# Opening three output tile pairs with products that need no forms, in a fused attention and gMLP kernel

## The chip, the cores and the metric

The kernel runs on one core of one Trainium2 chip. The metric is the time of one execution on the device in microseconds (us). TensorE is PE in the profile, VectorE is DVE, ScalarE is ACT, GpSimd is POOL, and SyncE is SP, whose queue issues most DMAs.

## The reference, cut to what matters

A layer-normalised dilated window attention comes first (its result, with the input added, is h), and then a gated MLP with a spatial product. The change touches the second block only.

```
z  = gelu(LN(h) @ w_in)                 # 2048 x 3584
z1 = z[:, :1792];  z2 = LN(z[:, 1792:])
g  = w_sp @ z2 + b_sp[:, None]          # w_sp 2048 x 2048, g 2048 x 1792
out = h + (z1 * g) @ w_out              # w_out 1792 x 1024
```

## The kernel before, in words

**Two halves.** The output's 2048 rows are worked in two halves (`pr` 0 and 1), each of 1024 rows. A half has two stages. The spatial stage (loop over `i`, L1454) makes z1 * g for seven feature tiles of 256 features and stores it in `zg`. The output stage (loop over `q`, L1584) multiplies `zg` by w_out for four pairs of 128-row tiles; `w` counts the pairs over both halves, so the first half has pairs 0 to 3.

**Seven products for eight.** Both stages use the Strassen-Winograd scheme: a product of two 2x2 block matrices by seven block products. For the output stage, A is `zg` (a11, a12, a21, a22: two row tiles by even and odd 128-feature groups) and B is the scaled w_out (B11, B12, B21, B22: even and odd feature groups by the two column halves). Two of the products need no forms, a11*B11 and a12*B21. The others need sums of blocks made by VectorE first: the S forms of a pair (`s_form`, L1437; S1 = a21+a22, S2 = S1-a11, S3 = a11-a21, S4 = a12-S2) and, once for all pairs, the T forms of the weights (`wform`, L1428; T1 = B12-B11, T2 = B22-T1, T3 = B22-B12 written over B12, T4 = B21-T2). Each block product is seven matmuls of 512 columns (`times`, L1272) into a PSUM bank. There are eight banks: two under the name `banka`, six under `bank`. The S forms share five buffers with the z forms, which are the same sums in the spatial stage (`z_form`).

**A pair.** In the pairs that run in seven products, PE makes k1 = a11*B11, k4 = S3*T3, k3 = S1*T1, k2 = S2*T2 in this order (L1627). ScalarE copies k1, k4 and k3 to SBUF as p1, p7 and p5 (L1636). PE then adds a12*B21 to k1, a22*T4 to k4 and S4*B22 to k3 (L1638 to L1641). So each of these three banks is written again after its copy. GpSimd adds p5 to p7 (L1643); VectorE makes the next pair's S forms, then u = k2 + p1 (L1662). GpSimd adds u to p7 (L1670). VectorE turns u into p1 and p5, with the row scale and the residual rows `hr` (L1671, L1672), and makes the four quarters of the output (L1680, L1683, L1685, L1693), which SP stores. I call these seven VectorE instructions the outputs. Between them stands work for the second half: the scaling of its two spatial weight tiles, 2 and 3 (`scale_raw`, L1175, half a tile at a time), and its forms (`t_forms`).

**Pair 0 of the first half.** It is the exception: at the start of the output stage no T forms exist, so it is made of eight products, four banks with 14 matmuls each (L1601 to L1606). VectorE makes all T forms and the S forms of pair 1 beside them and then four outputs (L1616). The last two feature groups of each bank come at the end, because tile 6 of the spatial stage is only just done.

**What comes ahead of it.** The seven weight tiles of w_out are scaled in place (`wout_scaled`, L1411). Tile 0 is scaled in spatial tile 5, after a matmul (`spread`, L1552) that spreads one factor over all partitions; tiles 1 to 4 are scaled by ScalarE and 5 and 6 by VectorE in spatial tile 6. Spatial tile 6 also scales both halves of spatial weight tile 2 on VectorE (L1533, L1534).

**What sets the order.** The order on every engine from here on is the order of the program's lines: each engine takes its own instructions strictly in that order, and semaphores hold it where data or a buffer is not ready.

Of the kernel before, what the change touches and what calls it, by code (L numbers as in the profile page):

```python
# [22 lines left out]
P = 128  # L23
# [109 lines left out]
def kernel(  # L133
# [1277 lines left out]
    def wout_scaled(fp):  # L1411
        w_ = wout_a[:, 2 * fp:2 * fp + 2, :] if fp < 4 else wout_b[:, 2 * fp - 8:2 * fp - 6, :]
        if fp < 5:
            A.activation(w_.bitcast(FP16), w_, ACTF.Copy, scale=kf[:, fp:fp + 1])
        else:
            V.tensor_scalar(w_.bitcast(FP16), w_, kf[:, fp:fp + 1], None, op0=ALU.mult)
# [18 lines left out]
    sforms = {}  # L1435
# [12 lines left out]
    for pr in range(NCH // 2):  # L1448
# [5 lines left out]
        for i in range(NQ):  # L1454
# [50 lines left out]
            if pr == 0:  # L1505
                if 1 <= i <= 4:
                    for t in (TPP + 2 * i - 2, TPP + 2 * i - 1):
                        row_sum(t, 0)
                        row_sum(t, 1)
                if i <= 3:  # L1510
                    load_wn2(TPP + 2 * i)
                for f in WSUM.get(i, ()):
                    wout_sum(f)
                if i == 6:
                    for fp in range(1, 5):
                        wout_scaled(fp)
            more = i + 1 < NQ
            if more:
                if n in (0, NQ):
                    z_form(n + 1, 3)  # L1520
                    z_form(n + 1, 1)
                if n == NQ:
                    bias_rows(1)
                if n == 0:
                    V.memset(ones[:], 1.0)
                    feature_scales()
            elif pr == 1:
                for m in (3, 1, 2, 4):
                    s_form(TPC, m, 0, NQ - 1)
            else:  # L1530
                for fp in range(5, NQ):
                    wout_scaled(fp)
                scale_raw(2, 0)  # L1533
                scale_raw(2, HK)  # L1534
# [13 lines left out]
            if n:  # L1548
                times(k3[:], slab(zs[n, 4]), slab(b22), False)
            if pr == 0 and i == 5:  # L1550
                spread = bank()
                T.matmul(spread[:, 0:2], ones[:], kb[0:1, 2:4], start=True, stop=True)  # L1552
            if more and n not in (0, NQ):
                z_form(n + 1, 3)
# [3 lines left out]
            if more and n not in (0, NQ):  # L1558
                z_form(n + 1, 1)
            if n == 3:  # L1560
                load_wout(4)
            nc.gpsimd.tensor_tensor(z22, p7[:], u[:], op=ALU.add)
            V.tensor_tensor(z21, k4[:], p1[:], op=ALU.add)
# [8 lines left out]
            if more and n not in (0, NQ):  # L1572
# [11 lines left out]
        for q in range(TPC):  # L1584
# [9 lines left out]
            if pr == 0 and q == 0:  # L1594
# [3 lines left out]
                wT12 = wtile([P, 2, NQ, CH], "woutT", "wB")[:].bitcast(FP16)  # L1598
                T1, T2 = pieces(wT12[:, 0]), pieces(wT12[:, 1])
                T4 = pieces(p2.tile([P, NQ, CH], FP16, name="wT4", tag="wn", bufs=1)[:])  # L1600
                accs = [(t, nh, bank_a() if (t, nh) == (0, 0) else bank()) for nh in (1, 0) for t in range(2)]  # L1601
                for f0, f1 in ((0, NF - 2), (NF - 2, NF)):
                    for t, nh, acc in accs:
                        for f in range(f0, f1):
                            T.matmul(acc[:], zg[:, f, (c1, c2)[t]:(c1, c2)[t] + P], wout_tile(f).bitcast(FP16)[:, nh * CH:(nh + 1) * CH],  # L1605
                                     start=(f == 0), stop=(f == NF - 1))  # L1606
                wform(T1, B12, B11)
                wform(T2, B22, T1)
                for m in (3, 1, 2, 4):
                    s_form(1, m)  # L1610
# [3 lines left out]
                for t, nh, acc in accs:  # L1614
                    hr, r_ = (h1, h2)[t], (r1, r2)[t]
                    V.scalar_tensor_tensor(hr[:, nh * CH:(nh + 1) * CH], acc[:], r_, hr[:, nh * CH:(nh + 1) * CH], op0=ALU.mult, op1=ALU.add)  # L1616
                for t, hr in ((t1_, h1), (t2_, h2)):
                    dma(out2d[t * P:(t + 1) * P, :], hr[:])
                continue
# [4 lines left out]
            p1, p7, p5, u = f32("p1", 3), f32("p7"), f32("p5"), f32("u2")  # L1624
            k1, k4, k3, k2 = bank_a(), bank(), bank(), bank()
# [4 lines left out]
            if q == 0:  # L1630
                for k_, a_, b_, _ in prods:
                    times(k_[:], a_, wslab(b_), True, 0, NQ - 1, NQ)
            for k_, a_, b_, p_ in prods:
                times(k_[:], a_, wslab(b_), True, NQ - 1 if q == 0 else 0, NQ, NQ)
                if p_ is not None:
                    A.copy(p_[:], k_[:])  # L1636
            cut = 3 * P
            times(k1[:], a12, wslab(B21), False, 0, NQ, NQ)  # L1638
            times(k4[:], a22, wslab(T4), False, 0, NQ, NQ)
            for lo, hi in ((0, cut), (cut, CH)) if end else ((0, CH),):  # L1640
                times(k3[:, lo:hi], S4, lambda k, lo=lo, hi=hi: wslab(B22)(k)[:, lo:hi], False, 0, NQ, NQ)  # L1641
# [27 lines left out]
            elif pr == 0:  # L1669
                nc.gpsimd.tensor_tensor(p7[:], p7[:], u[:], op=ALU.add)  # L1670
                V.scalar_tensor_tensor(p1[:], u[:], r1, h1[:, CH:D], op0=ALU.mult, op1=ALU.add)  # L1671
                V.scalar_tensor_tensor(p5[:], u[:], r2, h2[:, 0:CH], op0=ALU.mult, op1=ALU.add)  # L1672
# [6 lines left out]
            if pr or q < 3:  # L1679
                V.scalar_tensor_tensor(h1[:, 0:CH], k1[:], r1, h1[:, 0:CH], op0=ALU.mult, op1=ALU.add)  # L1680
            if pr == 0 and q < 3:
                (lambda: scale_raw(3, 0), lambda: t_forms(1, 0))[q - 1]()
# [9 lines left out]
            else:  # L1692
                V.scalar_tensor_tensor(h1[:, CH:D], k3[:], r1, p1[:], op0=ALU.mult, op1=ALU.add)  # L1693
                for t, hr in ((t2_, h2), (t1_, h1)):
                    dma(out2d[t * P:(t + 1) * P, :], hr[:])
            if pr == 0 and q == 1:
                scale_raw(3, HK)
# [32 lines left out]
```

## Time and profile before

| | us |
|---|---|
| median of 3 runs | 689.83 |
| lowest, highest | 689.65, 689.96 |
| profiled execution | 689.65 |
| its span in the trace | 687.9 |
| PE busy | 680.6 (99%) |
| DVE busy | 586.5 (85%) |
| ACT busy, POOL busy | 357.6, 170.2 |
| spatial stage of the first half, output stage of the first half | about 427 to 513, 513 to 557 |
| spatial and output stage of the second half | about 557 to 641, 641 to 685 |

In rows in order of time the columns are start, duration, engine, line, operation, what is written from what, its shape, and in square brackets how long the engine sat idle just before and who released it. A matmul's row is longer than its share of PE's time, because matmuls overlap: 379 ns is shown for one of 512 columns, and the next starts 216 ns after it. VectorE's rows overlap a little too, so I use the distance from one start to the next. The granted clock of PE is full throughout.

### The profile page before, as it was taken

To read this page: it belongs to the slowest core of one execution; us is meant where nothing else is said; L and a number is where in the kernel's file an instruction comes from. 1 tells how busy PE (TensorE), PEld (TensorE's weight loads), DVE (VectorE), ACT (ScalarE), POOL (GpSimd) and SP (SyncE) were. 2 spreads that over 40 slices of the span, in tenths; PEclk is the share of its full clock that TensorE was granted. 3 is DMA by queue.
4 is the path that set the end of the run, shared out by engine and by line. 5 is a ranking of instruction groups with operands and counts; after the bars stand their busy time and mean duration, and the time that the engine had idled before them with its cause. 6 is when DMAs were issued, how large, how long until landed. Compare 5 with 4: busy or idle time off the path is not lost.

```text
span 687.9 us, 9194 instructions
## 1 busy us (share of the span) xinstructions
PE 680.6 (99%) x3430; PEld 361.2 (53%) x3447; DVE 586.5 (85%) x742; ACT 357.6 (52%) x527; POOL 170.2 (25%) x145
## 2 busy tenths in 40 slices
PE   9999999999999999999999999999999999999997
PEld 6766666566645445444544467444444444444443
DVE  6899899998999989998897878997789999555565
ACT  4547652354229998764882556387771122324121
POOL 0100010010210101000120134474550426453442
PEclk9999999999999999999999999999999999999999
DMA  8979588567995469454483996999968215542031
GB/s 321 332 240 246 173 193 274 154 165 269 218 352 216 96 244 238 166 174 106 123 225 120 204 275 195 299 295 310 257 189 215 88 62 150 156 121 94 1 114 70
DMA packets 143933, 133.07 MB, mean 193 GB/s; under 512 B 68752, under 2 KB 115504, under 8 KB 143760
## 3 DMA queue, kind: packets, MB, share of 16 engines
q1 hardware_dynamic: 132720, 88.93, 45.1%
q0 software_dynamic: 8416, 34.80, 17.9%
q10 hardware_dynamic: 2752, 8.75, 3.8%
q8 instruction: 27, 0.44, 0.3%
q14 instruction: 18, 0.15, 0.1%
HBM read 75.25 MB, written 33.10 MB: 158 GB/s over the span
## 4 chain that ended last, share of the span: by engine, by line
PE 93%; DVE 2%; issue 2%; DMA 1%; POOL 1%; ACT 0%; DVEq 0%; POOLq 0%
PE bank L1274 22%; PE acc L468 22%; PE acc L800 14%; PE acc L868 11%; PE banka L1274 9%; PE acc L723 8%; PE acc L310 2%; PE acc L1040 1%; PE bank L1605 1%; DMA wout_a<-in_B_w_out_dram 1%; DVE zs L1209 1%; PE wps L232 1%; PE banka L1605 0%; PE banka L1040 0%; PE L L562 0%
## 5 line engine op out<-in xcount | busy, mean ns | idle before, releaser
L800 PE MATMUL acc<-win,hnT 128*128 128x512 bf16 (+1 forms) x501 | 97.4, 352 | 0.6
L800 PEld LDWEIGHTS <-hnT 128*128 128x128 bf16 x512 | 49.9, 98 | 47.4 <-issue 0.7
L532 DVE TENSOR_TENSOR prod<-qT,kT 128x4096 bf16<-128x4096 bf16 x32 | 72.7, 2282 | 1.6 <-ACT kT L474 1.3
L868 PE MATMUL acc<-hnT,win 128*128 128x512 bf16 x336 | 73.7, 379 | 0.0
L1274 PEld LDWEIGHTS <-zs 128*128 128x128 f16 x448 | 43.7, 98 | 54.4 <-DVE zs L1209 2.2
L479 ACT CAST stg<-acc 128x1024 bf16<-128x1024 f32 x36 | 36.4, 1012 | 61.6 <-PE acc L468 54.7
L468 PE MATMUL acc<-xnT,wk 128*128 128x512 bf16 x256 | 56.5, 379 | 0.0
L468 PE MATMUL acc<-xnT,wv 128*128 128x512 bf16 x256 | 56.4, 380 | 0.0
L723 PE MATMUL acc<-wo_sb,av_oT 128*128 128x512 bf16 x250 | 55.8, 379 | 0.3
L868 PEld LDWEIGHTS <-win 128*128 128x128 bf16 x336 | 32.7, 98 | 39.3 <-issue 0.5
L1274 PEld LDWEIGHTS <-z 128*128 128x128 bf16 x336 | 32.7, 98 | 39.1
L1274 PE MATMUL bank<-rawb,zs 128*128 128x512 f16 x224 | 52.6, 379 | 0.0
L1274 PE MATMUL bank<-form,zs 128*128 128x512 f16 x224 | 51.0, 379 | 1.2 <-DVE zs L1209 1.2
L1274 PE MATMUL banka<-rawa,z 128*128 128x512 f16 x224 | 52.0, 379 | 0.0
L468 PEld LDWEIGHTS <-wk 128*128 128x128 bf16 x256 | 36.5, 143 | 19.0 <-issue 0.8
L468 PEld LDWEIGHTS <-wv 128*128 128x128 bf16 x256 | 36.5, 144 | 18.6 <-issue 0.5
L468 PE MATMUL acc<-xnT,wq 128*128 128x512 bf16 x192 | 41.9, 379 | 0.0
L723 PEld LDWEIGHTS <-av_oT 128*128 128x128 bf16 x256 | 24.9, 98 | 29.9
L807 ACT ACTIVATE u<-acc 128x1024 bf16<-128x1024 f32 (+1 forms) x32 | 29.2, 911 | 19.6 <-PE acc L800 19.4
L536 DVE TENSOR_TENSOR prod<-prod 128x2048 bf16<-128x2048 bf16 x32 | 38.7, 1215 | 0.0
L1504 POOL TENSOR_TENSOR p<-p,p 128x512 f32<-128x512 f32 x14 | 22.4, 1602 | 53.6 <-ACT p L1488 48.5
L468 PEld LDWEIGHTS <-wq 128*128 128x128 bf16 x192 | 27.5, 143 | 13.9
(327 smaller groups left out, 1235.8 us busy)
## 6 DMA issues: line engine op xcount, KB each, us to landing
z<-z_d SPq DMA_DIRECT2D x28, 512.0 KB, 5.1
qkv_d<-stg SPq DMA_DIRECT2D x36, 256.0 KB, 4.7
wn<-in_B_w_sp_dram ACTq DMA_DIRECT2D x16, 512.0 KB, 5.1
z1c<-z_d SPq DMA_DIRECT2D x14, 512.0 KB, 4.8
z_d<-z1s SPq DMA_DIRECT2D x21, 256.0 KB, 2.6
z_d<-u SPq DMA_DIRECT2D x12, 448.0 KB, 2.6
av_y<-av_z POOLq DMA_DIRECT2D x4, 1024.0 KB, 9.8
av_oT<-av_zz POOLq DMA_DIRECT2D x4, 1024.0 KB, 15.1
```

The source lines that it names most:

```text
L232: T.matmul(wps[:], warm[:, 0:P], warm[:], start=True, stop=True)
L310: T.matmul(dst.rearrange("p (a b) -> p a b", b=P), wqs[:, kt, dl, :], xnT[0][:, lo:hi, kt, :], start=start, stop=stop)
L468: T.matmul(G[key][:, j, :].rearrange("p (a b) -> p a b", a=TPC), wv[:, kt, dl, :], xnT[c][:, :, kt, :], start=(kt == 0), stop=(kt == KT - 1))
L479: A.copy(stg[:], G[key][:])
L532: V.tensor_tensor(st["prod"][:], qT[:], kT[:, :, o:o + CH], op=ALU.mult)
L536: V.tensor_tensor(dst, p_[:, 0:4, :], p_[:, 4:8, :], op=ALU.add)
L723: T.matmul(st["acc", il][:, nh, :], oTs[c][:, dl, il * P:(il + 1) * P], wo_sb[:, dl, nh * CH:(nh + 1) * CH], start=(dl == 0), stop=(dl == ...
L800: T.matmul(accf[:, n0:n1], hnTs[c][:, il, kt, :], wins[hf][:, kt, n0:n1], start=(kt == 0), stop=(kt == KT - 1))
L807: A.activation(st["u", il][:, hf * 1024:hf * 1024 + wd], G["accz", c, il, hf][:].rearrange("p a b -> p (a b)")[:, 0:wd], ACTF.Gelu_apprx_t ...
L868: T.matmul(G["accy", c, fp][:, j, :].rearrange("p (a b) -> p a b", a=TPC), wt[:, kt, f0 * P:(f0 + 1) * P], hnTs[c][:, :, kt, :], start=(kt ...
L1274: T.matmul(dst, wts(k), mov(k), start=(first and k == 0), stop=(k == last - 1), skip_group_check=not first)
L1504: nc.gpsimd.tensor_tensor(p7[:], p7[:], p5[:], op=ALU.add)
```

## The change

Pair 0 of the first half is made of seven products like the others. To give PE something to do while the T forms are made, a11*B11 and a12*B21 of pairs 0, 1 and 2 run first (42 matmuls, three banks that stay open, with three copies p1); the last feature tile of a11*B11 comes after the first six of all three. Pair 0 then runs S1*T1, S2*T2, S4*B22, S3*T3, a22*T4; pairs 1 and 2 leave out the two products that they already have; pair 3 is as it was.

The rest moves around it. VectorE makes half of T1 (the part of w_out in the second buffer) inside spatial tile 6. Weight tile 4 is scaled by VectorE. The scaling of spatial weight tile 2 leaves spatial tile 6 and goes between the outputs of pair 0; those of tile 3 stay in pair 1. In each pair of the first half one quarter of the output moves between the making of p1 and p5. In spatial tile 5 the `spread` matmul goes ahead of a product, and in spatial tile 1 one z form, (2, 2) of the next tile, goes ahead of two other instructions.

```diff
@@ -1410,7 +1410,7 @@
 
     def wout_scaled(fp):
         w_ = wout_a[:, 2 * fp:2 * fp + 2, :] if fp < 4 else wout_b[:, 2 * fp - 8:2 * fp - 6, :]
-        if fp < 5:
+        if fp < 4:
             A.activation(w_.bitcast(FP16), w_, ACTF.Copy, scale=kf[:, fp:fp + 1])
         else:
             V.tensor_scalar(w_.bitcast(FP16), w_, kf[:, fp:fp + 1], None, op0=ALU.mult)
@@ -1432,7 +1432,8 @@
     def wslab(b):
         return lambda k: b[0][:, k, :] if k < 4 else b[1][:, k - 4, :]
 
-    sforms = {}
+    sforms, opened = {}, {}
+    NOPEN = 3
 
     def s_form(u, m, lo=0, hi=NQ):
         x0 = (u % TPC) * 2 * P
@@ -1512,7 +1513,7 @@
                 for f in WSUM.get(i, ()):
                     wout_sum(f)
                 if i == 6:
-                    for fp in range(1, 5):
+                    for fp in range(1, 4):
                         wout_scaled(fp)
             more = i + 1 < NQ
             if more:
@@ -1528,10 +1529,8 @@
                 for m in (3, 1, 2, 4):
                     s_form(TPC, m, 0, NQ - 1)
             else:
-                for fp in range(5, NQ):
+                for fp in range(4, NQ):
                     wout_scaled(fp)
-                scale_raw(2, 0)
-                scale_raw(2, HK)
             if n + 2 < 2 * NQ:
                 load_z2f(n + 2, 1)
             if n == 5:
@@ -1545,11 +1544,11 @@
             nc.gpsimd.tensor_tensor(u[:], u[:], bt2, op=ALU.add)
             if pr == 0 and i == 5:
                 wout_turned(turned[0:1, P:2 * P])
-            if n:
-                times(k3[:], slab(zs[n, 4]), slab(b22), False)
             if pr == 0 and i == 5:
                 spread = bank()
                 T.matmul(spread[:, 0:2], ones[:], kb[0:1, 2:4], start=True, stop=True)
+            if n:
+                times(k3[:], slab(zs[n, 4]), slab(b22), False)
             if more and n not in (0, NQ):
                 z_form(n + 1, 3)
             z11, z12 = zg[:, 2 * i, 0:CH], zg[:, 2 * i, CH:2 * CH]
@@ -1557,9 +1556,15 @@
             V.tensor_tensor(z11, k1[:], bt1, op=ALU.add)
             if more and n not in (0, NQ):
                 z_form(n + 1, 1)
+            if n == 1:
+                z_form(n + 1, 2)
             if n == 3:
                 load_wout(4)
             nc.gpsimd.tensor_tensor(z22, p7[:], u[:], op=ALU.add)
+            if n == NQ - 1:
+                wT12 = wtile([P, 2, NQ, CH], "woutT", "wB")[:].bitcast(FP16)
+                T1, T2 = pieces(wT12[:, 0]), pieces(wT12[:, 1])
+                wform(T1, wblk(0, 1), wblk(0, 0), (1,))
             V.tensor_tensor(z21, k4[:], p1[:], op=ALU.add)
             if more and n in (0, NQ):
                 z_form(n + 1, 4)
@@ -1569,7 +1574,7 @@
             if n not in Z1ACT:
                 z1_scaled(n)
             V.tensor_tensor(z12, k3[:], u[:], op=ALU.add)
-            if more and n not in (0, NQ):
+            if more and n not in (0, 1, NQ):
                 z_form(n + 1, 2)
             V.tensor_tensor(zg[:, 2 * i, :], zg[:, 2 * i, :], z1c[:, 0, :], op=ALU.mult)
             if more and n not in (0, NQ):
@@ -1595,50 +1600,58 @@
                 load_raw(3)
                 bias_in(1)
                 load_z1c(NQ + 1)
-                wT12 = wtile([P, 2, NQ, CH], "woutT", "wB")[:].bitcast(FP16)
-                T1, T2 = pieces(wT12[:, 0]), pieces(wT12[:, 1])
                 T4 = pieces(p2.tile([P, NQ, CH], FP16, name="wT4", tag="wn", bufs=1)[:])
-                accs = [(t, nh, bank_a() if (t, nh) == (0, 0) else bank()) for nh in (1, 0) for t in range(2)]
-                for f0, f1 in ((0, NF - 2), (NF - 2, NF)):
-                    for t, nh, acc in accs:
-                        for f in range(f0, f1):
-                            T.matmul(acc[:], zg[:, f, (c1, c2)[t]:(c1, c2)[t] + P], wout_tile(f).bitcast(FP16)[:, nh * CH:(nh + 1) * CH],
-                                     start=(f == 0), stop=(f == NF - 1))
-                wform(T1, B12, B11)
+                zz = zg[:].rearrange("p (k j) s -> p j k s", j=2)
+                first = [slab(zz[:, j, :, 2 * v * P:(2 * v + 1) * P]) for v in range(NOPEN) for j in range(2)]
+                for v in range(NOPEN):
+                    opened[v] = bank_a() if v < 2 else bank(), f32("p1", 3)
+                for lo, hi in ((0, NQ - 1), (NQ - 1, NQ)):
+                    for v in range(NOPEN):
+                        times(opened[v][0][:], first[2 * v], wslab(B11), True, lo, hi, NQ)
+                        if hi == NQ:
+                            A.copy(opened[v][1][:], opened[v][0][:])
+                for v in range(NOPEN):
+                    times(opened[v][0][:], first[2 * v + 1], wslab(B21), False, 0, NQ, NQ)
+                wform(T1, B12, B11, (0,))
+                s_form(0, 1)
                 wform(T2, B22, T1)
-                for m in (3, 1, 2, 4):
-                    s_form(1, m)
+                for m in (2, 4, 3):
+                    s_form(0, m)
                 wform(B12, B22, B12, (0,))
                 wform(B12, B22, B12, (1,))
                 wform(T4, B21, T2)
-                for t, nh, acc in accs:
-                    hr, r_ = (h1, h2)[t], (r1, r2)[t]
-                    V.scalar_tensor_tensor(hr[:, nh * CH:(nh + 1) * CH], acc[:], r_, hr[:, nh * CH:(nh + 1) * CH], op0=ALU.mult, op1=ALU.add)
-                for t, hr in ((t1_, h1), (t2_, h2)):
-                    dma(out2d[t * P:(t + 1) * P, :], hr[:])
-                continue
             zz = zg[:].rearrange("p (k j) s -> p j k s", j=2)
             a11, a12, a22 = slab(zz[:, 0, :, c1:c1 + P]), slab(zz[:, 1, :, c1:c1 + P]), slab(zz[:, 1, :, c2:c2 + P])
             S1, S2, S3, S4 = (slab(sforms[w, m]) for m in (1, 2, 3, 4))
             T3 = B12
-            p1, p7, p5, u = f32("p1", 3), f32("p7"), f32("p5"), f32("u2")
-            k1, k4, k3, k2 = bank_a(), bank(), bank(), bank()
+            k1, p1 = opened[w] if w in opened else (bank_a(), f32("p1", 3))
+            p7, p5, u = f32("p7"), f32("p5"), f32("u2")
+            k4, k3, k2 = bank(), bank(), bank()
             end = w == NT // 2 - 1
             prods = [(k1, a11, B11, p1), (k4, S3, T3, p7), (k3, S1, T1, p5), (k2, S2, T2, None)]
             if end:
                 prods = [prods[n_] for n_ in (0, 3, 2, 1)]
-            if q == 0:
+            elif w in opened:
+                prods = [prods[n_] for n_ in ((2, 3, 1) if w == 0 else (1, 2, 3))]
+            cut = 3 * P
+            def three():
+                for lo, hi in ((0, cut), (cut, CH)) if end else ((0, CH),):
+                    times(k3[:, lo:hi], S4, lambda k, lo=lo, hi=hi: wslab(B22)(k)[:, lo:hi], False, 0, NQ, NQ)
+
+            if w == TPC:
                 for k_, a_, b_, _ in prods:
                     times(k_[:], a_, wslab(b_), True, 0, NQ - 1, NQ)
             for k_, a_, b_, p_ in prods:
-                times(k_[:], a_, wslab(b_), True, NQ - 1 if q == 0 else 0, NQ, NQ)
+                if w == 0 and k_ is k4:
+                    three()
+                times(k_[:], a_, wslab(b_), True, NQ - 1 if w == TPC else 0, NQ, NQ)
                 if p_ is not None:
                     A.copy(p_[:], k_[:])
-            cut = 3 * P
-            times(k1[:], a12, wslab(B21), False, 0, NQ, NQ)
+            if w not in opened:
+                times(k1[:], a12, wslab(B21), False, 0, NQ, NQ)
             times(k4[:], a22, wslab(T4), False, 0, NQ, NQ)
-            for lo, hi in ((0, cut), (cut, CH)) if end else ((0, CH),):
-                times(k3[:, lo:hi], S4, lambda k, lo=lo, hi=hi: wslab(B22)(k)[:, lo:hi], False, 0, NQ, NQ)
+            if w:
+                three()
             if not end:
                 nc.gpsimd.tensor_tensor(p7[:], p7[:], p5[:], op=ALU.add)
             if q + 1 < TPC:
@@ -1669,6 +1682,10 @@
             elif pr == 0:
                 nc.gpsimd.tensor_tensor(p7[:], p7[:], u[:], op=ALU.add)
                 V.scalar_tensor_tensor(p1[:], u[:], r1, h1[:, CH:D], op0=ALU.mult, op1=ALU.add)
+                if q < 3:
+                    V.scalar_tensor_tensor(h1[:, 0:CH], k1[:], r1, h1[:, 0:CH], op0=ALU.mult, op1=ALU.add)
+                else:
+                    V.scalar_tensor_tensor(h1[:, CH:D], k3[:], r1, p1[:], op0=ALU.mult, op1=ALU.add)
                 V.scalar_tensor_tensor(p5[:], u[:], r2, h2[:, 0:CH], op0=ALU.mult, op1=ALU.add)
             else:
                 A.activation(p1[:], u[:], ACTF.Copy, scale=r1)
@@ -1676,10 +1693,10 @@
                 nc.gpsimd.tensor_tensor(p1[:], p1[:], h1[:, CH:D], op=ALU.add)
                 nc.gpsimd.tensor_tensor(p5[:], p5[:], h2[:, 0:CH], op=ALU.add)
                 nc.gpsimd.tensor_tensor(p7[:], p7[:], u[:], op=ALU.add)
-            if pr or q < 3:
+            if pr:
                 V.scalar_tensor_tensor(h1[:, 0:CH], k1[:], r1, h1[:, 0:CH], op0=ALU.mult, op1=ALU.add)
             if pr == 0 and q < 3:
-                (lambda: scale_raw(3, 0), lambda: t_forms(1, 0))[q - 1]()
+                (lambda: scale_raw(2, 0), lambda: scale_raw(3, 0), lambda: t_forms(1, 0))[q]()
             V.scalar_tensor_tensor(h2[:, 0:CH], k4[:], r2, (u if end else p5)[:], op0=ALU.mult, op1=ALU.add)
             if not end:
                 V.scalar_tensor_tensor(h2[:, CH:D], p7[:], r2, h2[:, CH:D], op0=ALU.mult, op1=ALU.add)
@@ -1690,11 +1707,12 @@
                     V.scalar_tensor_tensor(h1[:, CH + lo:CH + hi], k3[:, lo:hi], r1, p1[:, lo:hi], op0=ALU.mult, op1=ALU.add)
                     (dma if n else A.dma_start)(out2d[t1_ * P:(t1_ + 1) * P, CH + lo:CH + hi], h1[:, CH + lo:CH + hi])
             else:
-                V.scalar_tensor_tensor(h1[:, CH:D], k3[:], r1, p1[:], op0=ALU.mult, op1=ALU.add)
+                if pr or q < 3:
+                    V.scalar_tensor_tensor(h1[:, CH:D], k3[:], r1, p1[:], op0=ALU.mult, op1=ALU.add)
                 for t, hr in ((t2_, h2), (t1_, h1)):
                     dma(out2d[t * P:(t + 1) * P, :], hr[:])
-            if pr == 0 and q == 1:
-                scale_raw(3, HK)
+            if pr == 0 and q < 2:
+                scale_raw(2 + q, HK)
     sp_hand.__exit__(None, None, None)
     by_hand.__exit__(None, None, None)
```

## The prediction, made before the result

> **What bounds the kernel now.** I read the page's busy shares first, then the slices, then PE's own rows in order of time from 400 us to the end, and last the rows of VectorE between 513 and 575 us.
>
> ```profile
> PE 680.6 (99%) x3430; PEld 361.2 (53%) x3447; DVE 586.5 (85%) x742; ACT 357.6 (52%) x527; POOL 170.2 (25%) x145
> PE   9999999999999999999999999999999999999997
> DVE  6899899998999989998897878997789999555565
> ```
>
> PE has work in every slice, so a matmul taken out is time won only if PE does not wait instead. VectorE is full in slices 30 to 33 (516 to 585 us): the four output pairs of the first half and the start of the second half. After that it is half idle. So in just the stretch that the change rearranges two engines are full. PE waits there for nothing, but only because VectorE is a few us ahead. The waits view has one wait of PE from 390 us to the end:
>
> ```profile
> PE bank L1274 <- DVE zs L1209: 1.2, 1, 1.2
> ```
>
> Four groups of rows carry the sums. First, PE: 28 matmuls of a pair from 525.26 to 531.31 us, so 0.216 us each and 1.51 for a product of seven.
>
> ```profile
> 525.26 1.03 PE L1274 MATMUL banka<-wout_a,zg 128*128 128x512 f16 x4
> 531.31 1.03 PE L1274 MATMUL banka<-wout_a,zg 128*128 128x512 f16 x4
> 556.99 7.07 PE L1274 MATMUL banka<-rawa,z 128*128 128x512 f16 x32
> ```
>
> Second, the time from a product's last matmul to the next one in the same bank, with ScalarE's copy between them (first pair of the second half): last matmul starts 646.78, copy 647.20 to 647.78, next matmul 647.83, so 1.05 us from start to start.
>
> ```profile
> 646.78 0.38 PE L1274 MATMUL banka<-wout_b,zg 128*128 128x512 f16 x1
> 647.20 0.58 ACT L1636 COPY p<-banka 128x512 f32<-128x512 f32 x1 [11.66 <-PE banka L1274]
> 647.83 0.59 PE L1274 MATMUL banka<-wout_a,zg 128*128 128x512 f16 x2
> ```
>
> Third, VectorE's prices. Start to start, which is what a queue pays, a 2048-column weight form costs 1.14, a 1536-column one 0.87, four S forms 2.4, one output instruction 0.66, half a spatial tile (L1178) 2.2.
>
> ```profile
> 516.38 1.21 DVE L1430 TENSOR_TENSOR woutT<-wout_a 128x2048 f16<-128x2048 f16 x1
> 517.52 0.94 DVE L1430 TENSOR_TENSOR woutT<-wout_b 128x1536 f16<-128x1536 f16 x1
> 505.99 4.48 DVE L1178 TENSOR_TENSOR rawa<-rawa,rows 128x4096 f16<-128x4096 bf16 x2
> 543.42 1.14 DVE L1446 TENSOR_TENSOR sf<-zg 128x896 f16<-128x896 f16 x2
> ```
>
> Fourth, GpSimd beside it: of two equal instructions the one that meets GpSimd's add takes 1.75 us in place of 0.75.
>
> ```profile
> 534.02 0.75 DVE L1671 SCALAR_TENSOR_TENSOR p<-u,rinv_w,hr 128x512 f32<-128x512 f32 x1
> 534.13 1.77 POOL L1670 TENSOR_TENSOR p<-p,u 128x512 f32<-128x512 f32 x1 [1.96 <-DVE u L1662]
> 534.69 1.75 DVE L1672 SCALAR_TENSOR_TENSOR p<-u,rinv_w,hr 128x512 f32<-128x512 f32 x1
> ```
>
> **The change part by part.** Clock times are those of the profile before; the earlier gap is taken off at the end.
>
> *Matmuls.* Pair 0 takes 56 matmuls now and 49 after: 7 x 0.216 = **-1.51**.
>
> *The gap.* PE stands 1.18 us before 457.39, for z form (2,2) of L1209, which VectorE starts at 456.18. Moved up in tile 1 it follows form (2,1) and is done near 454.7; PE wants it at 456.2. **-1.18**. What is late next there: nothing, form (2,4) is ready 459.6 and wanted near 461.4. The sum over the tile z21 slips by 0.6, and VectorE has idle time in tiles 3 to 5.
>
> *Small moves.* The spread matmul goes ahead of eight others; its input is written by 497.61 and PE is there at 499.15, so no wait, and VectorE loses 0.82 idle, ScalarE starts scaling 0.8 sooner. Weight tile 4 goes from ScalarE (1.99) to VectorE (0.70): VectorE then ends at 506.8 and its next input, k2, is there at 508.2, so it is hidden; tile 4 is wanted by PE at 514. Scaling of spatial tile 2 (4.4) leaves tile 6, so u and GpSimd's three adds there run up to 2 us sooner, but zg still waits for PE's last product (ends 513.2): by the second half's same tile (product starts 639.87, z12 at 641.87, then two multiplications) zg is done at 515.45, not 516.4. The first T form's second part fits in VectorE's idle time before it. No DMA moves, except that outputs and the loads of hr behind them on SP shift with VectorE; hr(4), loaded behind pair 0's output near 541, is wanted near 553.
>
> *New waits of PE.* In the opening, two single matmuls follow a product's last one before the same bank is written again: 1.05 - 3 x 0.216 = **+0.40**. In pair 0, a22*T4 follows S3*T3 in the same bank at once: 1.05 - 0.216 = **+0.83**. Both are bounded below by 0 and above by 1.05.
>
> *VectorE's queue, the term that decides.* PE, never short of forms: opening 513.18 to 522.64 (42 matmuls and 0.40), pair 0 to 531.02 (35 and 0.83), pair 1 to 538.58, pair 2 to 546.1; pair 3 opens with a product that needs no forms and wants S3 at **547.7**. VectorE, from 515.45: rest of T1 1.14, S1 0.6, T2 2.0, three S forms 1.8, T3 2.0, T4 2.0 = 525.0. Three S forms of pair 1 end at 526.8. The fourth takes the buffer of pair 0's S4 (five buffers), which PE reads until 527.2, so 527.95. Then u, p1, h1's first half: 529.95. The next one, p5, writes what GpSimd's add reads, and that add waits for the copy of S3*T3 (529.47) and takes 1.2: p5 ends near 531.5. Half of tile 2 2.2; three outputs 2.0, the middle one behind GpSimd's second add (+0.6); the other half 2.2, with GpSimd's add for pair 1 in its way (+0.4): about 538.9. S3 of pair 2 is ready at 539.5, wanted at 538.58: **+0.9**. The next round (four S forms 2.4, seven outputs 4.6, two halves of tile 3 4.4 = 11.4, and one block of 0.5 and one of 0.5 by GpSimd) ends at 551.3, S3 of pair 3 is there at **551.9**; six products follow, 9.07, and the next row's matmuls (556.99 now) start at 561.0. That is **+4.0**, in which the -1.51, +0.40, +0.83 and +0.9 are contained and a second stall of about 3.4.
>
> Why so much: the queue before runs without idle from 516.4 to 574 and gets 8.8 us more (tile 2 4.4, four S forms 2.4, seven outputs for four 2.0), less 0.87 and 0.95 of a sooner start, while PE arrives sooner. Before, S3 of pair 3 was ready at 544.0 and wanted at 547.93: 3.9 us of lead, which does not cover it. Behind 561.0 both shift alike (forms of tile 8 were 1.2 ahead and still are), and from 588 us VectorE idles, so the loss is kept and does not grow.
>
> GpSimd's share is bounded both ways. Without a single block: the bare prices sum to 548.2 for S3 of pair 3, and the two waits by data (0.65 for the buffer, 0.85 for p5) make it 549.7. With each of its four adds in full (1.1 each, as 1.75 against 0.75 shows): 553. I take 551.9, because before each pair paid for both adds, and one output now stands between p1 and p5 in the add's way. The Trainium skill, page SBUF — State Buffer, section Who interferes with whom, says that GpSimd and a VectorE instruction with two SBUF inputs hold the shared port pair exclusively for a whole instruction, so the second blocks. The 1.75 beside the 1.77 above agrees; by that rule h1's half, with one input in PSUM, runs free beside the add, and a pair pays nearer 0.5 than 1.0 for it, which would put the end at the lower half of my bounds.
>
> **Sum.** 689.65 (profiled execution; its span is 687.9) + 4.0 - 1.18 = 692.5. The median of the runs shown is 0.18 above that execution, and I forecast on the median's scale: **692.6**.
>
> **The rivals.**
> *VectorE keeps ahead* (the other side, faster). PE then only has -1.51 - 1.18 + 0.40 + 0.83 = -1.46: 688.4. It decides if S3 of pair 3 is done by 547.7, 4.2 us sooner than I walk. For it: PE had no wait here before, and seven outputs may pack tighter with the new order. Against it: bare prices alone give 548.2.
> *VectorE is late, but GpSimd hardly blocks.* S3 at 549.7: 558.8 for the next row, +1.8 - 1.18 = +0.6, 690.4. For it: h1's half between p1 and p5. Against it: the adds still fall beside S forms and scalings, as a 4.40 us add at 541.29 shows.
> *The change does not do what it says at tile 1*: z form (2,2) is still late (ScalarE's copies run 1 us behind there, and GpSimd's adds lengthen forms to 1.04): the 1.18 stays, 693.8; with all adds in full, 695.
>
> **How the numbers follow.** The forecast, 691.2 to 694.4, has 0.59; the little-blocked queue, 688.5 to 691.2, 0.25; VectorE ahead, under 688.5, 0.12; more than 694.4, 0.04. A measurement of this kernel tells about 0.2% (1.4 us) from no change. So faster 0.12, same 0.25, slower 0.63. The range leaves out most of the faster case and the far end: 688.9 to 694.4.
>
> **What would show it.** PE's waits should name DVE sf L1446's form twice, near 538 and near 548 to 552, the second the longer; a wait of 0.8 for ScalarE's copy ahead of a22*T4 in pair 0; none at 457. VectorE should have no idle from 531 to 575. The row matmuls behind the four pairs should start near 560, against 556.99. I am wrong if PE does not wait before pair 3, or if VectorE idles while PE waits.

## The result and the profile after

The changed kernel takes **695.10 us** (median of 4 runs, 694.82 to 695.43), the kernel before 689.74 beside it (4 runs, 689.35 to 689.96). The ratio is 1.0079, 95% interval 1.0061 to 1.0096: 5.4 us slower. The direction was forecast, the size was not: 692.6 was forecast, and 695.10 is above the range. The profiled execution took 695.43 us with a span of 693.7, so 5.78 us more than the profiled execution before; the rows below explain that difference.

The page's busy shares and slices after:

```profile
PE 682.1 (98%) x3440; PEld 360.9 (52%) x3440; DVE 591.8 (85%) x750; ACT 357.2 (51%) x529; POOL 167.6 (24%) x147
...
PE   9999999999999999999999999999999799999997
...
DVE  6899899998999899998896878996989999555565
```

PE has a hole in slice 31, counted from 0 (538 to 555 us, of 17.3 each), where before it had none, though it was given less work. VectorE's slices look much as they did. A share of 85% hides that its work there has grown: its z form (8, 3) for the second half starts at 576.03, where it started at 570.63 before. PE's waits after 390 us, from the waits view (total, times, longest):

```profile
PE bank L1274 <- DVE sf L1447: 5.3, 2, 3.8
PE bank L1274 <- ACT p L1649: 0.7, 1, 0.7
PE banka L1274 <- ACT p L1612: 0.2, 1, 0.2
```

The wait of 1.2 for a z form is gone, and the forecast waits are there: the two for ScalarE's copies, and S3 twice, the second time the longer. The output stage's first row before, and then PE's rows after in order of time:

```profile
513.18 1.89 PE L1605 MATMUL bank<-wout_a,zg 128*128 128x512 f16 x8
```

```profile
511.90 1.03 PE L1274 MATMUL banka<-wout_a,zg 128*128 128x512 f16 x4
...
516.84 1.02 PE L1274 MATMUL banka<-wout_a,zg 128*128 128x512 f16 x4 [0.24 <-ACT p L1612]
...
528.25 1.67 PE L1274 MATMUL bank<-wT,zg 128*128 128x512 f16 x7 [0.67 <-ACT p L1649]
...
538.97 1.04 PE L1274 MATMUL bank<-wout_a,sf 128*128 128x512 f16 x4 [1.49 <-DVE sf L1447]
...
552.02 1.47 PE L1274 MATMUL bank<-wout_a,sf 128*128 128x512 f16 x4 [3.81 <-DVE sf L1447]
...
554.56 3.85 PE L1274 MATMUL bank<-woutT,sf 128*128 128x512 f16 x14
558.25 1.03 PE L1274 MATMUL banka<-wout_a,zg 128*128 128x512 f16 x4
...
562.78 7.07 PE L1274 MATMUL banka<-rawa,z 128*128 128x512 f16 x32
```

Read the starts. The output stage begins at 511.90, 1.28 sooner than before (513.18). The next row's matmuls begin 50.88 later, at 562.78, where they took 43.81 before. What was not forecast stands in the durations at 552.02 and 554.56: four matmuls in 1.47 where 1.03 is usual. From 552.02 to 558.25 PE runs 21 matmuls, at 0.216 each 4.54 us; it takes 6.23. The view by stretches (busy time of PE, PEld, DVE, ACT and POOL with counts, then PE's granted clock, DMA share, GB/s) shows it:

```profile
552.00:554.00 2.00, 1.98 (x6) 0.77 (x7) 1.79 (x4) 0.00 (x0) 0.00 (x0) 0.62 0.62 234
554.00:556.00 2.00, 2.00 (x6) 0.72 (x5) 1.96 (x4) 0.59 (x1) 1.30 (x1) 0.53 0.00 0
556.00:558.00 2.00, 2.00 (x11) 0.88 (x9) 2.00 (x3) 0.59 (x1) 0.87 (x2) 1.00 0.00 0
```

Behind the wait the granted clock is 0.62 and 0.53, and the view counts 6 matmuls in 2 us where it counts 11 at full clock (those that reach into a stretch are counted in it). So the wait is paid once as a wait and then again, 1.69 us, as a slow restart. The Trainium skill, page TensorE: Matmul & The Clock Gate, section What's actually happening, says that PE falls to half clock after an idle window of about 3.4 us and that this window runs freely. The 0.53 here agrees with the half; the length of wait that it takes is tested below.

The terms, start to start, on PE's clock of the profiled executions:

| term | forecast | measured |
|---|---|---|
| matmuls of pair 0 | -1.51 | -1.51 |
| copy wait in the opening (516.22 to 516.84, less 0.216) | +0.40 | +0.40 |
| copy wait in pair 0 | +0.83 | +0.83 |
| S3 of pair 2 (pair 1 ends 537.31, row at 538.97) | +0.9 | +1.66 |
| S3 of pair 3 (product before it ends 548.04, row at 552.02) | +3.4 | +3.98 |
| clock behind that wait | none | +1.69 |
| sum, 513.18 or 511.90 to the next row | +4.0 | +7.05 (rows: 50.88 - 43.81 = +7.07) |
| gap in spatial tile 1 and what lies ahead of the output stage | -1.18 | -1.28 |

7.07 - 1.28 is 5.79, the 5.78 of the profiled executions. Nothing is lost or won behind 562.78.

VectorE's side, its rows with GpSimd's beside them:

```profile
528.28 1.26 POOL L1656 TENSOR_TENSOR p<-p,p 128x512 f32<-128x512 f32 x1 [16.17 <-ACT p L1649]
529.57 1.86 DVE L1689 SCALAR_TENSOR_TENSOR p<-u,rinv_w,hr 128x512 f32<-128x512 f32 x1 [0.79 <-POOL p L1656]
529.62 1.27 POOL L1683 TENSOR_TENSOR p<-p,u 128x512 f32<-128x512 f32 x1
```

```profile
534.22 1.30 DVE L1702 SCALAR_TENSOR_TENSOR hr<-p,rinv_w,hr 128x512 bf16<-128x512 f32 x1
...
542.87 1.09 DVE L1689 SCALAR_TENSOR_TENSOR p<-u,rinv_w,hr 128x512 f32<-128x512 f32 x1
543.89 3.35 DVE L1178 TENSOR_TENSOR rawb<-rawb,rows 128x4096 f16<-128x4096 bf16 x1
...
551.35 1.15 DVE L1447 TENSOR_TENSOR sf<-zg 128x896 f16<-128x896 f16 x2
```

p5 of pair 0 waits 0.79 for GpSimd's add, as forecast (0.85), and then takes 1.86 for 0.75: GpSimd's second add starts 0.05 behind it and takes its usual 1.27, so it seems to go first. Half a tile 3 takes 3.35 for 2.27. An output (at 534.22) takes 1.30 for 0.74 and p5 of pair 1 1.09 for 0.75. These four make 3.1 us of blocking up to pair 3's S forms; I had put 2.0. Those forms start at 551.35 and S3, the first, takes 0.61, so it is written by 551.96.

### The profile page after: what moved, and what is told of

It reads as the page before. It is cut to its first block, busy times and chain, and to the rows that moved or that the text cites. A ratio compares the mean times of both kernels' runs of the same rounds, so it can differ in the third digit from the quotient of the medians.

```text
span 693.7 us, 9215 instructions
## 1 busy us (share of the span) xinstructions
PE 682.1 (98%) x3440; PEld 360.9 (52%) x3440; DVE 591.8 (85%) x750; ACT 357.2 (51%) x529; POOL 167.6 (24%) x147
## 4 chain that ended last, share of the span: by engine, by line
PE 92%; issue 4%; DVE 2%; DMA 1%; POOL 1%; ACT 0%; DVEq 0%; POOLq 0%
PE bank L1274 23%; PE acc L468 22%; PE acc L800 14%; PE acc L868 10%; PE banka L1274 9%; PE acc L723 8%; PE acc L1040 2%; PE acc L310 2%; PE acc L1004 0%; DMA xp<-in_A_x_dram 0%; PE banka L1040 0%; DMA hr<-h_d 0%; DVE rawb L1178 0%; PE L L562 0%; DMA out_dram<-hr 0%
## 5 line engine op out<-in xcount | busy, mean ns | idle before, releaser
L1274 PEld LDWEIGHTS <-sf 128*128 128x128 f16 x231 | 22.6, 100 | 33.4 <-DVE sf L1447 6.3
```

Source lines behind the costliest of these rows:

```text
L1274: T.matmul(dst, wts(k), mov(k), start=(first and k == 0), stop=(k == last - 1), skip_group_check=not first)
```

## The experiments

**Theory A**, formed from these rows: VectorE's queue is the whole loss. It was nearly full, it got more than it can do ahead of pair 3, GpSimd's adds lengthen it, and PE's falling clock adds to the wait that comes of it. The rivals differ from run to run and stand in each expectation: that the seven-product pair is at fault and not the scaling that moved, that the order within VectorE's queue is at fault and not its length, that the blocking by GpSimd matters little.

The medians of the kernel before, beside the runs, were 689.6 (27 runs; beside the gap alone, 14 more matmuls, the scaling back in tile 6, and no GpSimd adds) and 689.39 (7 runs; beside the other four).

### The gap alone

The kernel before with only the z form (2, 2) moved up in spatial tile 1.

```diff
             if more and n not in (0, NQ):
                 z_form(n + 1, 1)
+            if n == 1:
+                z_form(n + 1, 2)
...
-            if more and n not in (0, NQ):
+            if more and n not in (0, 1, NQ):
                 z_form(n + 1, 2)
```

> The kernel before with one edit: z form (2, 2) goes ahead of two instructions in spatial tile 1, and nothing else. Theory A (PE bounds everything there, and the 1.18 us wait is simply gone): 688.4, that is 1.2 to 1.4 us under the kernel before, with no wait of PE from 390 us on. Rival (the time is given back where VectorE has least lead, near spatial tile 8 of the second half, because VectorE's chain there does not start sooner): 689.0 to 689.7, with a new wait of PE near 570 to 590 us.

Measured: 688.12 (687.89 to 688.56, 11 runs), ratio 0.998 (0.9971 to 0.9989). The waits view has no wait of PE from 390 us to the end, and the next row's matmuls start 1.35 sooner than before's 556.99:

```profile
555.64 7.07 PE L1274 MATMUL banka<-rawa,z 128*128 128x512 f16 x32
```

This part of the change does what the prediction said. It is the fastest kernel of the study.

### The clock: 14 more matmuls in the wait, and 7

The changed kernel, with 14 matmuls that repeat a11*B11 into the bank of S3*T3 just ahead of it in pair 3. They change nothing in the output; they only keep PE at work in the wait.

```diff
+                if w == 3 and k_ is k4:
+                    for _ in range(2):
+                        times(k4[:], a11, wslab(B11), True, 0, NQ, NQ)
                 times(k_[:], a_, wslab(b_), True, NQ - 1 if w == TPC else 0, NQ, NQ)
```

> The changed kernel with 14 more matmuls, which only repeat a11*B11 into the bank that S3*T3 of pair 3 overwrites next, so they change no result and stand where PE waits 3.8 us. Theory A (after that wait PE's granted clock is about half for some 3 us, and this costs 1.7 us): with the wait cut to about 0.9 us the clock stays full, 21 matmuls behind it take 4.54 us in place of 6.23, and the time falls by 1.7 to 693.4 although PE does more work. Rival B (the matmuls are slow because the forms S1 and S2 arrive just in time, or because of what the other engines read meanwhile): the same slow matmuls, 695.1 or more.

Measured: 694.64 (694.34 to 694.87), 0.5 less than the change, where A said 1.7 less. PE's rows, and a stretch of the same view as above:

```profile
551.85 1.04 PE L1274 MATMUL bank<-wout_a,sf 128*128 128x512 f16 x4 [0.79 <-DVE sf L1447]
...
556.39 1.03 PE L1274 MATMUL banka<-wout_a,zg 128*128 128x512 f16 x4
...
577.30 1.90 PE L1274 MATMUL bank<-rawb,zs 128*128 128x512 f16 x8 [0.51 <-DVE zs L1209]
```

```profile
552.00:554.00 2.00, 2.00 (x10) 0.88 (x9) 1.79 (x4) 0.43 (x1) 0.00 (x0) 1.00 0.60 201
```

A's mechanism held: with a wait of 0.79 for 3.81 the clock stays at 1.00, the 21 matmuls take 4.54, and the next row's matmuls start at 560.92, 1.86 sooner. But 1.26 of it is given back behind that: 0.16 at a bank that VectorE seems to free late, 0.67 in spatial tile 8, where PE now waits for z form (8, 3), and 0.4 in tile 9 for form (9, 2). So the clock's drop costs 1.7 on the spot and only some 0.6 in the end. Behind it stands VectorE again, 25 us later. This is the first sign that tile 8, and not pair 3, decides. Part of that is GpSimd once more: with PE on time its add starts at 556.26 for 557.60, meets a form of the second half (3.35 for 2.28), and z form (8, 3) starts 0.54 later than in the change.

With 7 matmuls (`range(1)`):

> The changed kernel with 7 more matmuls (as in the run with 14) where PE waits 3.8 us, so that the wait is about 2.3 us. It is for the size of wait at which PE's granted clock drops: waits of 1.5 us left it full, one of 3.8 did not. Theory A (it takes more than 3 us of standing): the 21 matmuls behind the wait take 4.54 us, clock 1.00. Rival (any wait of 2 us does it): about 6 us for them, clock 0.6 or less.

Measured: 694.64 (one run). PE's wait is 2.30 here, and the clock stays full:

```profile
551.66 1.04 PE L1274 MATMUL bank<-wout_a,sf 128*128 128x512 f16 x4 [2.30 <-DVE sf L1447]
```

The 21 matmuls take 4.54 again (551.66 to 556.20), and tiles 8 and 9 take the win back in the same way. A's outcome came here; what it says of the length of wait is taken up again below, where a shorter one did bring the clock down.

### The scaling of spatial tile 2 back in tile 6

The changed kernel with one part undone.

```diff
                 for fp in range(4, NQ):
                     wout_scaled(fp)
+                scale_raw(2, 0)
+                scale_raw(2, HK)
...
-            if pr == 0 and q < 3:
-                (lambda: scale_raw(2, 0), lambda: scale_raw(3, 0), lambda: t_forms(1, 0))[q]()
+            if pr == 0 and 0 < q < 3:
+                (lambda: scale_raw(3, 0), lambda: t_forms(1, 0))[q - 1]()
...
-            if pr == 0 and q < 2:
-                scale_raw(2 + q, HK)
+            if pr == 0 and q == 1:
+                scale_raw(3, HK)
```

> The changed kernel with one part undone: both halves of spatial weight tile 2 are scaled in spatial tile 6 again, as before the change. Theory A (the 4.4 us that this move puts into VectorE's full queue are what PE waits for): S3 of pair 3 is ready near 546.7 against 551.9, PE waits under 1 us in all, no clock drop, the next row's matmuls start near 556 against 562.8, 688.1 to 689.5. Rival (the seven-product pair's own S forms and outputs, 4.4 us more, are already too much for VectorE): waits of 2 us or more remain before pair 2 or 3 or near tile 8, 690.5 to 692.

Measured: 690.82 (690.34 to 691.04, 10 runs), ratio 1.0016 (1.0007 to 1.0025). The rival's number came, not A's. PE's waits:

```profile
PE bank L1274 <- DVE sf L1447: 1.3, 1, 1.3
...
PE bank L1274 <- DVE zs L1209: 0.7, 2, 0.5
```

So the move of 4.4 us of scaling costs 4.3 us (695.10 to 690.82), nearly all of itself. But the rest of the change does not pay either: it is 2.7 above the gap alone. The rows say how. The next row's matmuls start at 557.10, 1.46 behind the gap alone; from there to the product of z form (8, 3) it takes 16.38 for 15.54, and a wait in tile 9, start to start, adds 0.40. Both are VectorE's: a pair in seven products saves PE 1.5 us, gives 0.40 and 0.83 back in copy waits, and puts four S forms and three outputs more, 4.4 us, into VectorE's full stretch. (The other moves of the change are still in this kernel, and none of them was run by itself but the gap and the output quarter.) A's cause holds here, but not its belief that the scaling was all of it.

### The scaling moved alone, in the kernel before

The reverse: the kernel before with pair 0 in eight products, and only the scaling of tile 2 moved, behind pair 0's four outputs.

```diff
-                scale_raw(2, 0)
-                scale_raw(2, HK)
...
                     dma(out2d[t * P:(t + 1) * P, :], hr[:])
+                scale_raw(2, 0)
+                scale_raw(2, HK)
                 continue
```

> The kernel before with one edit: the scaling of spatial weight tile 2 leaves spatial tile 6 and stands behind the four outputs of pair 0, which stays in eight products. Theory A (VectorE's queue from 516 us on is full and had 1.2 us of lead at tile 8): 4.4 us more, less 1.0 for the sooner end of tile 6, less the lead, so PE waits about 2.2 us in all, 691.4 to 692.4. Rival (4.4 us fit into VectorE's lead over PE, and it is the seven products that cost): 689.5 to 690.2.

Measured: 693.0 (692.87 to 693.33), ratio 1.0054 (1.0037 to 1.007): slower, as A said, and by more than it said. No product was taken out and no bank is written sooner, so the new waits are the moved scaling's alone (of the three for z forms one is the old 1.18 in tile 1):

```profile
PE bank L1274 <- DVE zs L1209: 2.6, 3, 1.2
PE bank L1274 <- DVE sf L1446: 1.4, 1, 1.4
```

The z form (8, 3) and the row of PE that holds its product, before (the product is the second eight of the row) and here:

```profile
570.63 0.67 DVE L1209 TENSOR_TENSOR zs<-z 128x1024 f16<-128x1024 bf16 x1
570.81 3.62 PE L1274 MATMUL bank<-rawb,zs 128*128 128x512 f16 x16
```

```profile
574.58 0.68 DVE L1209 TENSOR_TENSOR zs<-z 128x1024 f16<-128x1024 bf16 x1
575.32 1.90 PE L1274 MATMUL bank<-rawb,zs 128*128 128x512 f16 x8 [1.16 <-DVE zs L1209]
```

The form starts at 574.58 for 570.63 before, 3.95 later. In the kernel before it was 1.18 ahead of PE (started 570.63, product at 572.54, and 0.73 from the form's start to the product's where PE waits for it). 3.95 - 1.18 is 2.77, and the product starts 2.78 later, at 575.32. A wait in tile 9, for form (9, 2), adds 0.40: 3.2, which is the difference of the profiled executions (692.87 and 689.65).

### The second halves behind the S forms

The changed kernel with the second halves of tiles 2 and 3 scaled behind the next pair's S forms: the same work in an order that serves PE's nearest need first.

```diff
                     s_form(w + 1, m)
+                if pr == 0 and q in (1, 2):
+                    scale_raw(1 + q, HK)
...
-            if pr == 0 and q < 2:
-                scale_raw(2 + q, HK)
```

> The changed kernel with one reordering on VectorE and the same work: the second half of spatial weight tile 2 is scaled behind the S forms of pair 2, and that of tile 3 behind the S forms of pair 3, instead of ahead of them. Theory A (VectorE's queue as a whole is too long up to the forms of tile 8, at 576 us): PE's wait before pair 2 goes and that before pair 3 shrinks by about the 1.5 us that the earlier one took and more, but a wait for a z form of tile 8 appears, 693.2 to 694.6. Rival (only the order is wrong, there is room behind): 690.5 to 691.5, no wait near 576 us.

Measured: 694.77 (694.65 to 694.85), 0.3 below the change, just above A's range and 3 us above the rival's: that the order is at fault falls. PE's waits did not go, they moved:

```profile
PE bank L1274 <- DVE sf L1447: 2.0, 1, 2.0
PE bank L1274 <- DVE u L1677: 1.1, 1, 1.1
PE bank L1274 <- DVE zs L1209: 0.7, 2, 0.5
...
PE banka L1274 <- DVE hr L1663: 0.4, 1, 0.4
```

S3 comes sooner, but banks are freed later (u and hr are the instructions that read them out). And the z form (8, 3) starts at 576.57, and its product at 577.30: to the hundredth where they start with 14 matmuls in the wait, though PE's waits in pairs 2 and 3 differ between the two.

The clock fell here too, behind a wait of 2.05, shorter than the 2.30 that left it full: the 21 matmuls take 6.30 (549.65 to 555.95).

```profile
552.00:554.00 2.00, 2.00 (x6) 0.71 (x5) 2.00 (x2) 0.37 (x1) 0.00 (x0) 0.50 0.64 211
```

### Without GpSimd's adds

The changed kernel without GpSimd's two adds into p7 in pairs 0 to 2.

```diff
-            if not end:
+            if not end and (pr or q == 3):
                 nc.gpsimd.tensor_tensor(p7[:], p7[:], p5[:], op=ALU.add)
...
-                nc.gpsimd.tensor_tensor(p7[:], p7[:], u[:], op=ALU.add)
+                if q == 3:
+                    nc.gpsimd.tensor_tensor(p7[:], p7[:], u[:], op=ALU.add)
```

> The changed kernel without GpSimd's two adds into p7 in pairs 0, 1 and 2 of the first half, so the last quarter of the output of these pairs lacks p5 and u. Theory A (the adds block VectorE: 0.8 us wait by data, 1.1 and 0.6 in pair 0, 0.4 and 1.1 in pair 1): VectorE is 3.9 us sooner at S3 of pair 3, PE waits under 2.5 us there in place of 3.8 and not at all before pair 2, no clock drop, 689.5 to 690.5. Rival (VectorE's own instructions are the whole of it, blocks are hidden by waits that it has anyway): 693 or more.

Measured: 690.49 (690.03 to 690.7, 10 runs), ratio 1.0013 (1.0004 to 1.0022), 4.6 below the change, in A's range. p5 of pair 0 takes its bare price and waits for nothing:

```profile
528.37 0.74 DVE L1690 SCALAR_TENSOR_TENSOR p<-u,rinv_w,hr 128x512 f32<-128x512 f32 x1
```

S3 of pair 3 is written by 547.66, 4.3 sooner than in the change. 0.3 of that is an earlier start of the whole trace; the other 4.0 are the 3.1 of blocking and the 0.8 of p5's wait by data, read off the rows above. Even so PE waits 1.5 for it and 0.6 in tiles 8 and 9: bare prices alone are too long for the stretch, as the prediction's lower bound had it.

### The output quarter back behind p5

The changed kernel with the quarter of the output that the change put between p1 and p5 back in its old place: h1's first half in pairs 0 to 2, and in pair 3 (the lines at "...") its second half.

```diff
-                if q < 3:
-                    V.scalar_tensor_tensor(h1[:, 0:CH], k1[:], r1, h1[:, 0:CH], op0=ALU.mult, op1=ALU.add)
...
-            if pr:
+            if pr or q < 3:
                 V.scalar_tensor_tensor(h1[:, 0:CH], k1[:], r1, h1[:, 0:CH], op0=ALU.mult, op1=ALU.add)
...
```

> The changed kernel with one part undone: the quarter of the output that was put between p1 and p5 is back in its place behind p5 in the four pairs of the first half. Theory A (beside GpSimd's add this quarter, with an input in PSUM, is free, and p5 behind p1 at once pays the whole add): VectorE is 0.6 us later in each pair, 1.2 at S3 of pair 3, 696.0 to 697.2. Rival (GpSimd takes the same time from VectorE at another place): 694.8 to 695.4.

Measured: 696.44 (696.2 to 696.62), 1.3 above the change by the medians and 0.8 by the profiled executions, in A's range. p5 of pair 1 now meets GpSimd's add in full:

```profile
542.79 1.75 DVE L1685 SCALAR_TENSOR_TENSOR p<-u,rinv_w,hr 128x512 f32<-128x512 f32 x1
```

It took 1.09 in the change, and p5 of pair 0 waits 1.46 for data where it waited 0.79. It is the one move in the output pairs that was shown to pay. The Trainium skill, page SBUF — State Buffer, section Who interferes with whom, says that only a VectorE instruction that needs the shared ports is held up by GpSimd; the quarter, with one input in PSUM, took 0.74 beside the add at 542.21 in the change, and agrees.

### The runs on one scale

VectorE's z form (8, 3), with the product of PE that needs it (a computed start where that product did not wait: the start of the row that holds it and eight matmuls of 0.216):

| kernel | form starts | product starts | form's lead |
|---|---|---|---|
| before | 570.63 | 572.54 | 1.18 |
| the gap alone | 569.26 | 571.18 | 1.19 |
| no GpSimd adds | 572.06 | 572.80 | 0 |
| scaling back in tile 6 | 572.74 | 573.48 | 0 |
| scaling moved alone | 574.58 | 575.32 | 0 |
| change with 7 matmuls | 576.37 | 577.10 | 0 |
| change with 14 matmuls | 576.57 | 577.30 | 0 |
| second halves behind S forms | 576.57 | 577.30 | 0 |
| the change | 576.03 | 578.32 | 1.56 |
| quarter back behind p5 | 577.92 | 578.90 | 0.25 |

In the six kernels with no lead the product starts 0.73 or 0.74 behind VectorE's form, whatever PE did in the pairs ahead of it. The change and the last kernel have a lead left, and in both PE lost 1.69 to its clock just before; 1.69 sooner, PE would have had to wait in both.

## Why the prediction missed

**What held.** The mechanism and the sign: PE's work got less, VectorE's queue got longer where it was full, and PE waits for S3 before pairs 2 and 3, the second wait the longer. The 0.216 of a matmul, the 1.05 from product to product around a copy, the gap in tile 1, the buffer wait (0.63 for 0.65) and p5's wait (0.79 for 0.85) came as worked out, and so did the moves that were costed at nothing: no wait of PE stands at `spread`, at weight tile 4 or at the first T form.

**The step that failed is VectorE's queue.** "The next round ... ends at 551.3, S3 of pair 3 is there at 551.9" rests on 2.0 of blocking by GpSimd, put into the walk up to there; the rows have 3.1, and without those adds the form is there 4.0 sooner. The output stage begins 1.28 sooner after, so on its clock 551.9 is 550.6, and S3 was written by 551.96: 1.3 late, 1.1 of it blocking and the rest bare prices a little above those that were added up. That made the two waits 1.66 and 3.98 in place of 0.9 and 3.4, +1.3 together. The reason given for the low value, one output between p1 and p5, was true of p5 in pair 1 (1.09), and the order is worth 0.8 to 1.3 us. But the adds that miss p5 fall on what runs next: an output (1.30) and half a tile (3.35). The bound with every add in full, 553, is 551.7 on the clock of after: it was 0.2 from what came, and the choice of 551.9 below it was the error. (One add in full is 1.0 by the two rows given, 1.75 and 0.75, and not 1.1.) The queue before, read as one "without idle from 516.4", did stand once, 0.40 at 524.39.

**"Behind 561.0 both shift alike (forms of tile 8 were 1.2 ahead and still are)"** fell as well. PE had 3.9 us of lead on S3 before but 1.18 in tile 8, and that smaller lead is the one the queue has to respect. With PE at full clock the z form (8, 3) is late, and PE pays 1.26 from there on, 0.67 of it for that form (14 matmuls in the wait). In the change itself this cannot be seen, because PE had been slowed.

**The clock was not in the sum.** The drop behind the 3.8 wait cost 1.69 at the place. Of the 2.9 between 692.5 and the profiled 695.43, the rows give 1.3 to the queue's two waits and 1.69 to the clock. Yet with the clock kept, the time falls by only some 0.6; the difference comes back as the waits behind it. So most of the miss, some 2.3 of 2.9, is VectorE's queue, and the clock's own share is 0.6 or less. One of the change's four executions has a mean granted clock of 1.000, the others 0.997 and 0.998 (a drop as in the profiled one makes 0.998); it took 695.20, between the others' 694.82 and 695.43.

**The rivals.** "VectorE keeps ahead" is out: PE stood 3.98 at S3 of pair 3. "Hardly blocks" is refuted by the kernel without the adds: all the adds of three pairs have to go to come to 690.49, the time that this rival gave to little blocking. "The gap not closing" is refuted by 688.12; that its figure with all adds in full, 695, lies at the measured time is luck, for the gap did close and the clock's drop took its place in the sum.

**The parts, added up from medians.** 689.6 before; the gap -1.5 (688.12); the seven-product pair with all that goes with it +2.7 (690.82); the scaling of tile 2 moved into the pairs +4.3 (695.10). The last price holds behind the others; moved alone, the scaling cost 3.6 (689.39 to 693.0).

**What stays open** is what makes the clock fall. A wait of 2.05 brought it down, with a wait of 1.1 some 8 us ahead of it; 2.30 did not in its one execution, with 1.5 some 13 us ahead; 3.8 did in the profiles of two kernels. A rule of one whole idle window of about 3.4 us does not fit the 2.05, which is shorter than the window. Two things point at phase. Read in stretches of 0.5 us, the half clock lasts 3.4 us each time (552.5 to 555.9 in the change, 550.8 to 554.2 with the second halves behind the forms, 552.7 to 556.1 with the quarter back), and it begins 0.5, 1.1 and 0.1 us after PE has started again, not at a fixed distance. And one execution of the change in four, by its mean clock of 1.000, seems to have had no such drop, though the kernel is the same. The free-running window that the Trainium skill's page TensorE: Matmul & The Clock Gate describes in its section What's actually happening would do that, but no run here shifted the phase alone. No run joined the gap alone with the moved output quarter either.

## What to carry to other kernels

When work moves onto an engine that is not the bound, ask for that engine's smallest lead over the whole full stretch, and not for its lead at the first place where someone waits. Here a delay of 3.95 us against the smallest lead found, 1.18, cost 2.8 at that place, and a reordering that served the first wait only moved the waits. Look at that lead stage by stage; an 85% share said nothing of it. A part of a change that closes a gap of its own may be the part to keep: 688.12 against 695.10.

## What the runs showed of the hardware

- PE's granted clock fell to about half (0.50 to 0.62 in stretches of 2 us) for 3.4 us behind waits of 2.05 and 3.8 us in the midst of a busy kernel, and a wait of 2.30 in another execution left it full; 21 matmuls then took 6.2 to 6.3 us for 4.54.
- A VectorE instruction that starts 0.05 us ahead of GpSimd's add can still be the one that is held up: p5 at 529.57 took 1.86 for 0.75, and the add at 529.62 its usual 1.27.
- A bank written again right behind ScalarE's copy of it cost 1.05 us from matmul to matmul in the opening and in pair 0, as in the second half of the kernel before.
